# Two-scale attention with a gated convolution on one core: the mask of the local scores as eight products on the scores' own tiles

## The chip, the core and the metric

The kernel runs on one core of one Trainium2 chip. A core has a matrix engine (TensorE, PE in the rows; its weight loads are PEld), VectorE (DVE), ScalarE (ACT), GpSimd (POOL) and SyncE (SP), which issues most transfers. Each engine works through its own queue in order and waits on semaphores for the others. Two on-chip memories matter: SBUF, from which all engines read, and PSUM, into which TensorE writes and from which VectorE and ScalarE read. The metric is the device time of one execution in microseconds (us).

## The reference: what is computed

Batch 8, 8 heads, 576 positions, head width 64. Each position attends to its neighbours nearer than four (local), and, over means of four positions, to the whole sequence (coarse). Their sum is multiplied with `w_val`, gated by a causal convolution of five taps, and multiplied with `w_out`.

```python
out_d = sm_attn(q_d, k_d, v_d)                  # q, k, v as means over 4 positions
out_up = np.repeat(out_d, factor, axis=2)
mask = np.abs(pos[:, None] - pos[None, :]) < factor
scores = scale * np.matmul(q, k.transpose(0, 1, 3, 2))
scores = np.where(mask, scores, -1000000000.0)
...
x = out_up + out_local                          # heads side by side: 512 columns
gate = 1.0 / (1.0 + np.exp(-gate_pre))          # gate_pre: 5 taps of x along the sequence
return gate * (x @ w_val) @ w_out
```

## The kernel before

The work is cut into 32 pairs: eight batches with four pairs of heads each (p = 4 * batch + pair). A pair passes through these steps, by the names that stand in the rows. `sl`: local scores on TensorE. The sequence is cut into 20 blocks of 29 queries, each with its 35 keys; a product has 64 rows (one head's width) and 29 columns of weights, so it takes a 64x32 tile of the array, eight of which stand side by side: two halves of the rows (one per head) and four groups of 32 columns. The scores lie in two PSUM banks (b = 0, 1), four groups of 32 partitions each. In the program there are 40 f32 products; the profile shows each as two rows, 80 in all. Then `mx`, `ex`, `sm`, `rs` (row maximum, difference, sum, reciprocal on VectorE, the exponential on ScalarE) and `pexp` (normalization, in two halves, on VectorE or GpSimd), `tl` (transposes on TensorE, copied to `pt` by ScalarE) and `x` (local output on TensorE). The coarse way: `half` and `qs` (sums over four positions for the first two batches, VectorE or GpSimd), `sd` (coarse scores), `cmx`, `cbi`, `pd`, `cs`, `crs` (softmax), `tc` (transposes, copied to `pdt`), `odp` (coarse output) and `od`. `xt` adds both. `xhs` and `xls` are x split into a high and a low part, `gp` is the convolution (a first tap on ScalarE, four on VectorE) and its gate. The projections work in blocks of 504 columns of the joined batches: `val` (16 groups per block, of three 504-column products: high by high, high by low, low by high), `h` (gate times val), `hhl` (h split in two), `out`, `ob` and the transfer to `out_t`. The weights come as f64 bit fields and are split on the chip (`raw`, `a_v`, `a_o`, `wl`).

The mask is added by TensorE itself. `lay` (L714 to L721) opens a pair's scores: for each of the two banks one bf16 product of the whole array, the identity (`ident_b`, 128x128) with 175 columns of `mask_b`, starts the sum in PSUM with -1e9 where a key doesn't count and 0 elsewhere. `mm` (L723) then adds the 80 score rows. The mask table (`_band_mask`) has one row per partition of the scores: query j of block parity e stands in row 32 * (hd + 2e) + j.

The order of all instructions is written out while the program is built. `tensor_order` (L488) gives TensorE's list from the tables `START`, `START3`, `START4` and `STEADY`, one entry per step, where `P` is one group of three projection products and a stroke behind a name means the pair before. `Planner` then plays the list through with a duration for every step (the numbers in each `op(...)`, `RESULT`, `switch`), takes a later entry of the list where the first one isn't ready, chooses VectorE, ScalarE or GpSimd where a step may run on several, and lets each engine's instructions be issued in the order that came out. A step that has `cols` may get dummies ahead of it (`keep_warm`, L589: bf16 products of a constant into a PSUM bank that is written anew afterwards), as many as `keep_busy` (L430) counts. Transfers into SBUF are sent by SP (`send`, L608), each waiting for the fourth before it (`PACE = 4`), in the order of `EARLY` at first. `QKSPLIT = 1` cuts q and k of pair 0 into two transfers (`qk_in`, L655).

## Time and profile before

| | before |
|---|---|
| runs without a profile, us | 375.63, 373.29, 371.87 (median 373.29) |
| profiled execution, us | 373.75 |
| its span (first to last instruction), us | 371.5 |
| busy in the span: TensorE, VectorE, ScalarE, GpSimd, us | 358.9, 304.9, 247.5, 91.1 |
| TensorE's granted clock, mean over the span | 0.999 |
| instructions | 14101 |

Busy time is what an engine's own instructions cover. Products on TensorE are pipelined and their ends are modelled, so rows of one engine overlap, and the step from one start to the next says more than a duration. Times in the rows count from the start of the span.

### The profile page before, as it was taken

The page shows a single profiled execution, that of the slowest core. Times are in us where ns is not written, and L with a number is a line of the kernel's source. Part 1 is how long each engine was busy: PE and PEld are TensorE (multiplying, and loading weights), DVE is VectorE, ACT ScalarE, POOL GpSimd, SP SyncE. Part 2 cuts the span into 40 slices and gives each one's busy share as a digit, 9 for nine tenths or more (in the row PEclk, how much of TensorE's full clock was granted, in tenths as well). Part 3 has the DMA queues.
Part 4 walks back from the last instruction along what each step waited for, and adds up shares of the span by engine and source line. Part 5 has one row for each costly group of instructions (what it writes and reads, how often), then busy time and mean ns, then how long its engine had stood idle before and what let it go on. Part 6 is the DMA issues. An engine that isn't in the chain of part 4 may idle for free.

```text
span 371.5 us, 14101 instructions
## 1 busy us (share of the span) xinstructions
PE 358.9 (97%) x6020; PEld 286.0 (77%) x6020; DVE 304.9 (82%) x673; ACT 247.5 (67%) x664; POOL 91.1 (25%) x116
## 2 busy tenths in 40 slices
PE   7899899998999999999999999999999999999996
PEld 4677676776777777777778787777777778778996
DVE  3988999998999989997999799879997999570520
ACT  2898798967875949674777587857874767422221
POOL 4211225741462116102522052203100320000000
PEclk9999999999999999999999999999999999999999
DMA  7899999999989969995799879892345101102012
GB/s 248 246 278 297 332 220 231 268 249 292 285 187 275 255 197 235 200 280 199 197 207 232 279 187 203 228 239 68 101 154 160 37 3 59 56 0 85 28 49 79
DMA packets 23550, 68.97 MB, mean 186 GB/s; under 512 B 2880, under 2 KB 8768, under 8 KB 23488
## 3 DMA queue, kind: packets, MB, share of 16 engines
q1 hardware_dynamic: 18592, 50.42, 42.0%
q0 software_dynamic: 4608, 17.50, 26.0%
q8 instruction: 47, 0.77, 0.9%
q10 hardware_dynamic: 288, 0.16, 0.2%
q14 instruction: 15, 0.12, 0.1%
HBM read 58.63 MB, written 9.44 MB: 183 GB/s over the span
## 4 chain that ended last, share of the span: by engine, by line
PE 75%; DMA 11%; DVE 9%; ACT 3%; issue 2%; POOL 0%; SPq 0%; DVEq 0%; ACTq 0%
PE val L1119 8%; PE val L1121 8%; PE val L1120 8%; PE out L1119 8%; PE out L1120 8%; PE out L1121 8%; DMA vg<-in_vg 6%; PE x L939 5%; PE sl L732 5%; PE odp L981 5%; PE tl L889 5%; PE tc L912 4%; DMA qk<-in_qk 3%; DVE gp L1030 3%; PE sd L809 3%; DMA out_t<-ob 2%
## 5 line engine op out<-in xcount | busy, mean ns | idle before, releaser
L1030 DVE SCALAR_TENSOR_TENSOR gp<-xt,cw,gp 128x576 f32<-128x576 f32 x128 | 106.0, 836 | 2.6 <-ACT gp L1024 2.4
L1119 PE MATMUL val<-xhs,wh_v 128*128 128x504 f32 (+1 forms) x160 | 63.2, 395 | 0.0
L1121 PE MATMUL val<-xls,wh_v 128*128 128x504 f32 (+1 forms) x160 | 59.6, 372 | 0.1
L1120 PE MATMUL val<-xhs,wl_v 128*128 128x504 f32 (+1 forms) x160 | 59.5, 372 | 0.0
L1119 PE MATMUL out<-hhl,wh_o 128*128 128x504 f32 (+1 forms) x144 | 57.6, 400 | 0.1
L1121 PE MATMUL out<-hhl,wh_o 128*128 128x504 f32 (+1 forms) x144 | 54.8, 380 | 0.0
L1120 PE MATMUL out<-hhl,wl_o 128*128 128x504 f32 (+1 forms) x144 | 54.7, 380 | 0.0
L1147 DVE SCALAR_TENSOR_TENSOR h<-gp,val 128x288 f32<-128x288 f32 (+6 forms) x64 | 26.7, 447 | 18.8 <-PE val L1121 18.5
L1211 ACT ACTIVATE ob<-out 128x504 f32<-128x504 f32 (+2 forms) x40 | 22.0, 551 | 24.7 <-PE out L1121 11.4
L832 ACT ACTIVATE pd<-sd,cbi 112x144 f32<-112x144 f32 x96 | 35.4, 380 | 1.6 <-DVE cbi L825 1.6
L1121 PEld LDWEIGHTS val<-xls,wh_v 128*128 128x128 f32 x160 | 30.1, 188 | 5.6 <-DVE xls L1013 0.5
L1119 PEld LDWEIGHTS val<-xhs,wh_v 128*128 128x128 f32 x160 | 30.1, 188 | 4.1 <-issue 0.2
L1120 PEld LDWEIGHTS val<-xhs,wl_v 128*128 128x128 f32 x160 | 30.2, 189 | 3.5
L1119 PEld LDWEIGHTS out<-hhl,wh_o 128*128 128x128 f32 x144 | 27.2, 189 | 5.8 <-issue 1.0
L1167 POOL TENSOR_TENSOR hhl<-h,hhl 128x504 fp32r<-128x504 f32 x15 | 19.2, 1278 | 49.9 <-DVE gp L1030 23.6
L1024 ACT ACTIVATE gp<-xt,cw 128x576 f32<-128x576 f32 x32 | 24.8, 776 | 9.5 <-DVE h L1147 7.4
L1121 PEld LDWEIGHTS out<-hhl,wh_o 128*128 128x128 f32 x144 | 27.1, 188 | 5.1
L1120 PEld LDWEIGHTS out<-hhl,wl_o 128*128 128x128 f32 x144 | 27.2, 189 | 3.8
L732 PEld LDWEIGHTS sl<-qk 64*29 64x29 f32 x2560 | 24.8, 103 | 6.9 <-issue 1.6
L1161 ACT CAST hhl<-h 128x504 fp32r<-128x504 f32 (+2 forms) x44 | 22.1, 521 | 11.9 <-DVE h L1147 11.9
L1009 ACT CAST xhs<-xt 128x576 fp32r<-128x576 f32 (+4 forms) x40 | 22.3, 577 | 11.7 <-DVE xt L950 11.4
L950 DVE TENSOR_TENSOR xt<-x,od 128x290 f32<-128x290 f32 x64 | 26.3, 450 | 4.6 <-PE x L939 3.3
(96 smaller groups left out, 731.5 us busy)
## 6 DMA issues: line engine op xcount, KB each, us to landing
qk<-in_qk SPq DMA_DIRECT2D x31, 586.0 KB, 5.6
qs<-in_qkr POOLq DMA_DIRECT2D x18, 576.0 KB, 7.9
vw<-in_vw SPq DMA_DIRECT2D x32, 320.0 KB, 5.9
out_t<-ob SPq DMA_DIRECT2D x32, 252.0 KB, 5.2
vs<-in_vgr POOLq DMA_DIRECT2D x21, 320.0 KB, 7.5
qs<-in_qkr SPq DMA_DIRECT2D x6, 576.0 KB, 7.4
vs<-in_vgr SPq DMA_DIRECT2D x7, 320.0 KB, 5.4
raw_v<-in_w_val SPq DMA_DIRECT2D x4, 512.0 KB, 6.0
```

Of the source, the lines that this page charges most:

```text
L732: nc.tensor.matmul(out=sc[32 * qd : 32 * qd + BQ, b, m * KW : (m + 1) * KW], lhsT=t[r, 0, 3 + blk : 3 + blk + BQ], rhs=t[r, 1, blk : blk + ...
L832: nc.scalar.activation(out=s["pd"][:, g], in_=s["sd"][:, g], func=AF.Exp, scale=1.0 / 128.0, bias=s["bi"][:, g : g + 1], accum_out=s["csm" ...
L950: nc.vector.tensor_tensor(out=s["xt"][:, 4:].rearrange("p (m a j r) -> p a m j r", m=NPR, a=2, r=2)[:, par], in0=s["x"][par].rearrange("p ...
L1009: nc.scalar.copy(out=xhs[:, c, g : g + t - f], in_=s["xt"][:, 4 + f : 4 + t])
L1024: nc.scalar.activation(out=s["gp"], in_=s["xt"][:, 4 : 4 + S], func=AF.Copy, scale=cw[:, c, 4:5])
L1030: return nc.vector.scalar_tensor_tensor(out=s["gp"], in0=s["xt"][:, k : k + S], scalar=cw[:, c, k : k + 1], in1=s["gp"], op0=ALU.mult, op1 ...
L1119: nc.tensor.matmul(out=o, lhsT=wh[:, d, col], rhs=his[d], start=d == 0, stop=False)
L1120: nc.tensor.matmul(out=o, lhsT=wl[:, d, col], rhs=his[d], start=False, stop=False)
L1121: nc.tensor.matmul(out=o, lhsT=wh[:, d, col], rhs=los[d], start=False, stop=d == NC - 1)
L1147: nc.vector.scalar_tensor_tensor(out=t["h"][:, cs], in0=st[b * NC + c]["gp"][:, f:e], scalar=1.0, in1=box["o"][:, cs], op0=ALU.add, op1=AL ...
L1161: nc.scalar.copy(out=t["hh"][:, cuts[n]], in_=t["h"][:, cuts[n]])
L1211: nc.scalar.mul(t["ob"][:, cs], box["o"][:, cs], 0.5)
```

## The change

The two mask products of the whole array become eight of a 64x32 tile each: every tile that will hold scores is started by a product of 64 rows of the identity, 32 of its columns, with 175 columns of the mask. The rows of the identity are chosen so that each tile takes its 32 mask rows out of its own half of the partitions, and the table of the mask is laid out anew for that. Mask and scores become one step (`sl`) in place of two (`mk`, `sl`), in the planner's tables too, with the duration 800 in place of 172 and 711 and 88 weight loads in place of 82. q and k of pair 0 come in one transfer.

```diff
-QKSPLIT = 1
+QKSPLIT = 0
...
-STEADY = "odp'' x'' sd tc1' tc0' P P P P mk sl tl1' tl0' P P P P"
+STEADY = "odp'' x'' sd tc1' tc0' P P P P sl tl1' tl0' P P P P"
...
-        def lay():
-            s["sc"] = sc = ps.tile([P, 2, 512], F32, tag="s", name=f"sl{p}", bufs=SB)
+        def mm():
+            t = s["qk"]
+            sc = ps.tile([P, 2, 512], F32, tag="s", name=f"sl{p}", bufs=SB)
             keep_warm(sc[:, 0])
             for b in range(2):
-                nc.tensor.matmul(
-                    out=sc[:, b, 0:n], lhsT=ident_b, rhs=mask_b[:, n * b : n * b + n], start=True, stop=False
-                )
-
-        def mm():
-            t, sc = s["qk"], s["sc"]
+                for qd in range(4):
+                    r = (LO, HI)[(qd + b) % 2]
+                    rows = r.start + 32 * (qd // 2)
+                    nc.tensor.matmul(
+                        out=sc[32 * qd : 32 * qd + 32, b, 0:n],
+                        lhsT=ident_b[r, rows : rows + 32],
+                        rhs=mask_b[r, n * b : n * b + n],
+                        start=True,
+                        stop=False,
+                    )
...
-            ("mk", p), "PE", 172, lay, [("qk", p)], banks=[("s", [("sub", p)])], cols=(350, 350), loads=2,
+            ("sl", p), "PE", 1300 if p < QKSPLIT else 800, mm, [("qk", p)],
+            banks=[("s", [("sub", p)])], cols=(1180, 350), loads=88,
         )
-        op(("sl", p), "PE", 1200 if p < QKSPLIT else 711, mm, [("qk", p), ("mk", p)], cols=(1050, 0), loads=80)
...
-                rows = [32 * (hd + 2 * e) + j for hd in range(2)]
+                rows = [32 * (e + 2 * half) + j for half in range(2)]
```

What this does to the order, at three places. First, TensorE at pair 10, as at nearly every pair behind it: the last projection product, mask, scores, transposes of the pair before. Before:

```order
L1121 MATMUL val1_2_1942<-xls_90,wh_v_96 128x504
L719 LDWEIGHTS ident_b_79
L719 MATMUL sl10_1976<-mask_b_91,ident_b_79 128x175
L719 LDWEIGHTS ident_b_79
L719 MATMUL sl10_1976<-mask_b_91,ident_b_79 128x175
L732 MATMUL sl10_1976<-qk10_1397 29x35 x40
L889 MATMUL tl9_1_2027<-ident_77,pexp1_81 128x128 x2
```

And of the change, where the pair of a load and a product stands eight times (once here):

```order
L1126 MATMUL val1_2_2011<-xls_90,wh_v_96 128x504
L723 LDWEIGHTS ident_b_79
L723 MATMUL sl10_2050<-mask_b_91,ident_b_79 32x175
...
L737 MATMUL sl10_2050<-qk10_1532 29x35 x40
L894 MATMUL tl9_1_2111<-ident_77,pexp1_81 128x128 x2
```

Six loads and six products more stand in a pair; what stands around them is the same. At pairs 17, 21 and 29 a group of the projection stood between mask and scores, and no longer does.

Second, TensorE in the opening, where the coarse and the local output of pair 3 are computed (`odp3`, `x3`; `vg3` is the part of v that they need, `const` marks a dummy). Before, with four dummies ahead of `odp3` and two ahead of `x3` (one of each here):

```order
L1121 MATMUL val0_1_898<-xls_90,wh_v_96 128x504
L809 MATMUL sd5_914<-qs1_722 64x144 x6
L592 LDWEIGHTS const-bfloat16-1.0
L592 MATMUL odp3_929<-const-bfloat16-1.0 128x144
...
L981 MATMUL odp3_929<-pdt3_853,vg3_540 64x144 x16
L592 LDWEIGHTS const-bfloat16-1.0
L592 MATMUL x3_964<-const-bfloat16-1.0 128x290
...
L939 MATMUL x3_964<-pt3_866,vw3_486 64x58 x20
```

And of the change, with twenty dummies ahead of `odp3` (one here):

```order
L1126 MATMUL val0_1_913<-xls_90,wh_v_96 128x504
L944 MATMUL x3_946<-pt3_892,vw3_513 64x58 x20
L592 LDWEIGHTS const-bfloat16-1.0
L592 MATMUL odp3_981<-const-bfloat16-1.0 128x144
...
L986 MATMUL odp3_981<-pdt3_879,vg3_581 64x144 x16
L894 MATMUL tl4_0_1034<-ident_77,pexp0_80 128x128 x3
L592 LDWEIGHTS const-bfloat16-1.0
L592 MATMUL sd5_1039<-const-bfloat16-1.0 128x350
L814 MATMUL sd5_1039<-qs1_742 64x144 x6
```

The coarse scores of pair 5 have gone from ahead of `odp3` to behind it, `x3` from behind it to ahead. In the whole program there are 90 dummies in place of 68, all but a few of them ahead of pair 5.

Third, GpSimd from pair 5 to pair 6 (its DMA rows are transfers that add into `qs` and `vs`). Before:

```order
L1100 TENSOR_TENSOR wl_o_99<-a_o2_1068,wh_o_98 128x512
L769 TENSOR_TENSOR pexp1_81<-ex1_83,rs5_1187 64x2x5x35
L634 DMA vs2_1039<-in_vgr 80x1024
L698 TENSOR_TENSOR half7_1_1303<-qk7_922 128x288
L634 DMA qs2_957<-in_qkr 128x1152
L1167 TENSOR_TENSOR hhl0_1_1294<-h0_1_1178,hhl0_1_1294 128x504
L634 DMA vs2_1039<-in_vgr 80x1024
L1167 TENSOR_TENSOR hhl0_2_1406<-h0_2_1391,hhl0_2_1406 128x504
L769 TENSOR_TENSOR pexp0_80<-ex0_82,rs6_1441 64x2x5x35
```

Of the change:

```order
L1105 TENSOR_TENSOR wl_o_99<-a_o2_1202,wh_o_98 128x512
L699 TENSOR_TENSOR qs1_742<-half7_1_1209 128x144
L634 DMA qs2_1063<-in_qkr 128x1152
L1172 TENSOR_TENSOR hhl0_1_1375<-h0_1_1207,hhl0_1_1375 128x504
L634 DMA vs3_1324<-in_vgr 80x1024
L774 TENSOR_TENSOR pexp0_80<-ex0_82,rs6_1424 64x2x5x35
```

The normalization of pair 5 and the low part `hhl0_2` are on VectorE now. In the same way the low parts of x of pairs 0 and 5 and the half normalization of pair 9 have gone to VectorE, that of pair 8 to GpSimd. After pair 9 half a normalization of pairs 10, 17, 19, 21 and 29, the coarse normalizations of pairs 13, 22, 24 and 25 and the low part of x of pair 20 have gone to VectorE, and four low parts of h, half a normalization of pair 23 and a coarse one (pair 11) have left it, net.

## Rows read from the trace of the kernel before

**Rows 1.** Windows by stage: stretch, us, busy (instructions), clock, DMA share, GB/s.

```profile
5.00:33.00 28.00, 24.20 (x595) 17.95 (x579) 24.30 (x62) 22.75 (x67) 4.74 (x6) 1.00 0.96 275
33.00:93.00 60.00, 55.54 (x1077) 42.45 (x1071) 58.07 (x124) 49.32 (x128) 24.02 (x29) 1.00 1.00 270
93.00:310.00 217.00, 217.00 (x3916) 172.17 (x3914) 198.00 (x444) 153.49 (x428) 58.70 (x62) 1.00 0.73 189
```

**Rows 2.** Timeline of TensorE, pair 20: start, us, engine, line, what, count, [idle before].

```profile
199.91 0.33 PE L719 MATMUL sl<-mask_b,ident_b 128*128 128x175 bf16 x2
200.17 0.89 PE L732 MATMUL sl<-qk 64*29 64x35 f32 x80
201.00 0.77 PE L889 MATMUL tl<-ident,pexp 128*128 128x128 f32 x5
...
203.87 0.39 PE L1120 MATMUL out<-hhl,wl_o 128*128 128x504 f32 x1
204.10 0.39 PE L1121 MATMUL out<-hhl,wh_o 128*128 128x504 f32 x1
204.42 0.71 PE L981 MATMUL odp<-pdt,vs 72*64 72x144 f32 x8
```

**Rows 3.** TensorE's groups by form: count | busy us, mean ns | idle before.

```profile
L809 PE MATMUL sd<-qs 64*64 64x144 f32 x384 | 17.3, 289 | 1.9 <-DVE qs L699 0.9 <-DVE ex L747 0.7 <-DVE xt L950 0.3
...
L592 PE MATMUL odp<-const-bfloat16-1.0 128*128 128x144 bf16 x12 | 1.5, 231 | 0.0
```

**Rows 4.** Timeline of TensorE: the coarse scores of pairs 26 and 27.

```profile
253.66 0.92 PE L809 MATMUL sd<-qs 64*64 64x144 f32 x24
254.51 0.39 PE L912 MATMUL tc<-ident_s,pd 112*72 112x112 f32 x2
```

**Rows 5.** Timeline of SP: issues of q and k of pair 0, and of v.

```profile
0.74 1.30 SPq L609 DMA_DIRECT2D qk<-in_qk  x2
...
5.35 0.34 SPq L609 DMA_DIRECT2D vg<-in_vg  x1
```

**Rows 6.** The page's transfers: count, KB each, median us from issue to landing.

```profile
qk<-in_qk SPq DMA_DIRECT2D x1, 296.0 KB, 3.9
```

**Rows 7.** Timeline of TensorE in the opening.

```profile
4.66 1.30 PE L732 MATMUL sl<-qk 64*29 64x35 f32 x80
...
43.84 0.43 PE L592 MATMUL odp<-const-bfloat16-1.0 128*128 128x144 bf16 x4
44.20 2.18 PE L981 MATMUL odp<-pdt,vg 72*64 72x144 f32 x32
...
68.01 0.31 PE L592 MATMUL out<-const-bfloat16-1.0 128*128 128x350 bf16 x1 [0.65 <-DVE h L1147]
...
90.43 0.32 PE L719 MATMUL sl<-mask_b,ident_b 128*128 128x175 bf16 x2 [0.57 <-ACT pd L832]
...
92.89 0.30 PE L592 MATMUL tc<-const-bfloat16-1.0 128*72 128x336 bf16 x1 [0.53 <-ACT pt L894]
```

**Rows 8.** Timeline of VectorE in the opening.

```profile
33.26 0.46 DVE L698 TENSOR_TENSOR half<-qk 128x288 f32<-128x288 f32 x1 [1.03 <-DMA qk<-in_qk]
...
78.51 1.56 DVE L1030 SCALAR_TENSOR_TENSOR gp<-xt,cw,gp 128x576 f32<-128x576 f32 x1
```

**Rows 9.** VectorE's groups by form, columns as in rows 3.

```profile
L1030 DVE SCALAR_TENSOR_TENSOR gp<-xt,cw,gp 128x576 f32<-128x576 f32 x128 | 106.0, 836 | 2.6 <-ACT gp L1024 2.4
L769 DVE TENSOR_TENSOR pexp<-ex,rs 64x350 f32<-64x350 f32 x51 | 27.8, 545 | 1.1
...
L1013 DVE TENSOR_TENSOR xls<-xt,xhs 128x576 fp32r<-128x576 f32 x18 | 13.6, 754 | 3.9 <-ACT xhs L1009 3.9
...
L1167 DVE TENSOR_TENSOR hhl<-h,hhl 128x504 fp32r<-128x504 f32 x9 | 6.0, 671 | 0.7 <-ACT hhl L1161 0.7
```

**Rows 10.** Timeline of GpSimd beside the tap at 78.51 us of rows 8.

```profile
78.02 1.43 POOL L1013 TENSOR_TENSOR xls<-xt,xhs 128x576 fp32r<-128x576 f32 x1 [0.65 <-DVE xls L1013]
```

More of the change, by code (lines that the diff above doesn't have):

```diff
@@ L110 @@
 COLS = 3400
-START = "mk sl tl0' tl1' sd tc1' tc0' odp' x'"
-START3 = "tl1' sd mk sl tl0' tc0' tc1' x' odp'"
-START4 = "mk sl tc0' tl1' P tl0' sd tc1' odp' x' P P P"
-STEADY = "odp'' x'' sd tc1' tc0' P P P P mk sl tl1' tl0' P P P P"
+START = "sl tl0' tl1' sd tc1' tc0' odp' x'"
+START3 = "tl1' sd sl tl0' tc0' tc1' x' odp'"
+START4 = "sl tc0' tl1' P tl0' sd tc1' odp' x' P P P"
+STEADY = "odp'' x'' sd tc1' tc0' P P P P sl tl1' tl0' P P P P"
 AHEAD = "0.0 0.1 1.0 1.1"
@@ L173 @@
 class Planner:
[L177 removed]
+    RESULT = {"sl": 223, "sd": 211, "tc": 198, "tl": 200, "odp": 213, "x": 345}
     PIECE = {"DVE": 105, "ACT": 151, "POOL": 200, "PE": 0}
@@ L225, in lat @@
         return self.CROSS[e].get(to, 200)
-    SHAPE = {"P": "full", "mk": "full", "tc": "turn", "tl": "turn", "odp": "half", "x": "four", "sd": "four", "sl": "eight"}
+    SHAPE = {"P": "full", "tc": "turn", "tl": "turn", "odp": "half", "x": "four", "sd": "four", "sl": "eight"}
     def switch(self, a, b):
```

1 line of the change is left out of this document (removed).

## Prediction, written before the changed kernel ran

> **What bounds the kernel now.** I read the busy times by stage first [rows 1]. From 93 to 310 us TensorE is busy in all of 217.00 us, at a granted clock of 1.00, which is its 2.4 GHz level; VectorE is busy for 198.00 of them, ScalarE for 153.49. TensorE sets the pace there: what an edit takes out of its stream comes off the end, until VectorE's 19 us of slack are used up. From 33 to 93 us it is mixed: VectorE 58.07 of 60 us, the DMA engines at a share of 1.00, TensorE 55.54. From 5 to 33 us the DMA share is 0.96 and no compute engine is full. The change therefore has a place that I can price (TensorE's stream from about 53 us on, where the weights' products have begun to fill it) and a place that I can only bound (the opening).
>
> Then the timeline of TensorE around one pair's scores [rows 2]. Rows overlap, since the end of a product is modelled, so I price by start to next start. The two mask products start at 199.91, the scores at 200.17, the transposes at 201.00: 0.26 us for the mask, 0.83 us for the 80 score rows. A 504-column product takes 0.23 us to the next one (203.87 to 204.10), which is 0.45 ns per column, so the mask's two times 175 columns are 0.158 us. The remaining 0.10 of the 0.26 is the turn from the whole array to tiles of 64x32. The same turn shows elsewhere: the last 504-column product before the coarse output takes 0.32 us to its successor (204.10 to 204.42) and not 0.23, so 0.09.
>
> **The change part by part.**
>
> *The mask, per pair.* Out go two whole-array products, 0.158 us. In come eight products of 175 columns, each on its own 64x32 tile. The turn of 0.10 us stays: it moves from behind the mask to ahead of it. So a pair gains 0.158 less what the eight cost. No row of before has a bf16 product on such a tile, so I bound it. If the tiles work at once, the eight cost the longer of one stream (175 x 0.45 ns = 0.079 us) and eight issues at the scores' own pace (0.83 us / 80 = 10.3 ns each, 0.082 us). If four work at once they cost 0.158, and the gain is nil; if two, 0.316; if one, 0.63.
> Which is nearer? An f32 product of 144 columns has a modelled time of 289 ns, a bf16 dummy of as many columns 231 ns [rows 3]: f32 needs 58 ns more, hence about twice the 0.45 ns, some 0.85 ns per column. The coarse scores run 24 products of 144 columns on four 64x64 tiles between 253.66 and 254.51 [rows 4]: one after the other that would be 24 x 0.122 = 2.9 us, and it is 0.85, so about 3.5 of four tiles work at once. The local scores are 80 x 35 x 0.85 ns = 2.4 us in 0.83, about three at once, held back by their 10.3 ns per issue. Long streams fill their tiles, and 175 columns are long. I take 0.09 us: the gain is 0.07 us a pair, with ends 0.079 and 0.
> It counts for pairs 5 to 31, whose scores stand where TensorE is full or nearly so: 27 x 0.07 = 1.9 us, ends 0 and 2.1. For pairs 0 to 4 it disappears in waits.
> The Trainium skill, "TensorE: Matmul & The Clock Gate", section "Back-to-back issue gap", has a floor of about 25 ns from one product's start to the next however few the columns. By it the eight would cost 0.20 us and each pair lose 0.04, some 1.1 us in all, which is a time of 375.7 with the opening's term below. The scores' 10.3 ns per product on the same eight tiles speak against it here.
>
> *One piece for mask and scores.* Both pieces waited for the same tile of q and k, and nothing new is waited for. In the place where a projection stood between mask and scores (three later pairs), one more turn of 0.09 us falls away; I leave these 0.3 us in the margin. Behind the piece the transposes and projections wait for nothing else. The 12 more instruction rows per pair on TensorE cost their issue, which the 10.3 ns hold already.
>
> *Pair 0's q and k in one transfer.* The first half's issue starts at 0.74 us and the two issues take 1.30; the first transfer of v goes out at 5.35, on the second half's landing [rows 5]. The second half (296 KB) landed 3.9 us after its issue [rows 6], at about 5.3. One transfer has the same bytes, starts at 0.74 and lands between 4.7 (an issue of 0.6 us saved) and 5.4. Scores of pair 0 start before that today, at 4.66, but take 1.30 us [rows 7], since their last part waits for the second half; in one go they are 0.9 us from landing. So their end moves by -0.3 to +0.3 us. The three transfers behind it on SP's queue are issued 0.6 us earlier or more; from the first of v on each waits for the fourth before it, and that lands as today. I price it at 0: VectorE waits for a later q and k at 33.26 after 1.03 us idle [rows 8], so what is won or lost before is swallowed there; ends -0.3 and +0.5.
>
> *The moved order.* The opening's order is another on every engine, up to about pair 10. Two things can be counted.
> First, dummies ahead of the coarse output of pair 3: 20 products of 144 columns now, 4 before. Four took 0.36 us (43.84 to 44.20) [rows 7], so 16 more are 1.4 us, less two dummies that fall away ahead of x3 (0.35 at most): +1.1 us if TensorE could have worked there, 0 if it waits anyway. I take the middle, +0.5.
> Second, VectorE takes work from GpSimd. Up to pair 9, net: two low parts of x (0.75 us each), one normalization (0.55) and one low part of h (0.67) [rows 9], 2.7 us; the sums of q and k that change sides nearly cancel. But GpSimd's work holds VectorE up: a convolution tap, 0.84 us in the mean [rows 9], took 1.56 us at 78.51, beside a low part of x on GpSimd from 78.02 [rows 8, 10]. Two low parts of x less on GpSimd give back about 1.4 us. Net 1.3 us, of which a part falls before 33 us, where VectorE has 3.7 us free. I take +0.4 for the end; ends 0 and 2.7. On the other side the new order may lose gaps of the old: TensorE waited 0.65 us at 68.01, 0.57 at 90.43, 0.53 at 92.89 [rows 7], 1.75 us.
> After pair 9 VectorE gets some 2.2 us more in the same way (four normalizations, three coarse ones and a low part of x, less four low parts of h), against 19 us of slack; I price that at 0, and if the slack is in the wrong place it is 2.2 us.
>
> **Sum.** 373.75 us for the profiled execution (span 371.5 and 2.25 around it): -1.9 (mask) + 0 (transfer) + 0.9 (opening) = 372.75. That execution is 0.46 us above the median of the runs shown, 373.29; from the median it would be 372.3. I forecast **372.5 us**. The ends together: 373.75 - 2.1 - 1.75 - 0.3 = 369.6, and 373.75 + 1.1 + 2.7 + 0.5 = 378.05 with nothing gained.
>
> **The rivals.**
> *The opening costs more than the mask gives.* Place: pairs 3 to 9. For it: VectorE is at 58.07 of 60 us there, it gets more work, and the 20 dummies are on TensorE's queue whether or not it waits. Against: GpSimd's hold-ups shrink with the work. Price +2.5 to +3.8 (both terms whole): 373.75 - 1.9 + 2.5 = 374.4, to 375.7.
> *The opening gains.* The old gaps of 1.75 us close and the dummies hide: 373.75 - 1.9 - 1.75 = 370.1, to 371.5 with half of it.
> *The mask products do not run eight at once: slower than before.* Place: every pair's scores. With two at once each pair loses 0.158 us, 27 x 0.158 = 4.3: 373.75 + 4.3 + 0.9 = 379; one at a time 0.47 x 27 = 12.8: 387. It decides from 0.158 us for the eight on (no gain) and is visible above 0.30 us. For it: no bf16 product on tiles is in the trace, and the local scores fill only three of eight tiles. Against: the coarse scores fill 3.5 of four.
> *The change does nothing:* four at once, gain nil, opening as forecast: 374.6.
>
> **How the numbers follow.** Chances: forecast (371.5 to 374.0) 0.52, opening dearer 0.18, opening gains 0.17, mask not at once 0.08, no gain 0.05. A measurement of this kernel can tell about 1% (3.7 us) from no change: 369.6 to 377.0. Below lies the far end of the opening's gain, 0.09; above the mask rival and the far end of the dear opening, 0.13; between 0.78. The range 369.8 to 377.2 leaves out the mask rival, 0.08, and the two far ends, about 0.1.
>
> **What would show it.** Mask start to first score start plus the turn ahead: 0.18 to 0.20 us if I am right, over 0.26 if not. Scores 0.83 as before. Steps of TensorE from pair to pair after 93 us shorter by 0.07. TensorE gapless from pair 10 on. Dummies before the output of pair 3: whether TensorE's rows before them show a wait. The mask of pair 20, at 199.91 before [rows 2], tells opening and mask together: fifteen pairs' gain of 1.05 against 0.9 of the opening puts it at 199.8. A wait of TensorE on VectorE after 110 us would make the sum wrong, and so would mask products that start 20 ns or more apart.

## The result, and the profile after

| | before | after |
|---|---|---|
| median of the runs timed beside each other, us | 374.28 (371.87 to 375.77, 6 runs) | 370.21 (369.77 to 370.98, 6 runs) |
| ratio, with its 95% interval | | 0.9896 (0.9856 to 0.9936) |
| profiled execution, its span, us | 373.75, 371.5 | 370.79, 369.0 |
| busy: TensorE, VectorE, ScalarE, GpSimd, us | 358.9, 304.9, 247.5, 91.1 | 356.8, 305.3, 247.4, 82.4 |
| instructions | 14101 | 14510 |

The change is worth 1.0%, 4.07 us between the medians. The forecast was 372.5 with a range of 369.8 to 377.2; the time lies at the lower end of the range, below the forecast's own case (371.5 to 374.0), and the gain is about four times the 1.0 us that was forecast (373.75 to 372.75). Here and below a median is over all executions of a kernel, a ratio over those within 1.5% of its fastest.

Busy time by stage, to be held against [rows 1] (span of the stretch, then busy time and instructions of PE, PEld, DVE, ACT, POOL, granted clock, DMA share, GB/s):

```profile
5.00:33.00 28.00, 25.31 (x669) 19.17 (x670) 25.82 (x69) 22.47 (x66) 2.84 (x5) 1.00 0.99 291
33.00:93.00 60.00, 57.17 (x1103) 43.97 (x1101) 57.59 (x127) 50.24 (x132) 21.70 (x27) 1.00 1.01 264
93.00:310.00 217.00, 215.26 (x4093) 171.60 (x4092) 200.06 (x451) 155.08 (x433) 54.21 (x54) 1.00 0.72 190
```

Two things stand out. TensorE is busier in the opening (57.17 of 60 us, 55.54 before; about 1 us of that is dummies, of which twenty take 1.41 us below where four took 0.36). And it is no longer gapless behind 93 us: 215.26 of 217.00.

The timeline of TensorE shows both the mask and the gaps (start, duration, engine, line, operation; in brackets the idle time before and what ended it):

```profile
17.94 0.63 PE L737 MATMUL sl<-qk 64*29 64x35 f32 x49 [0.91 <-issue]
...
23.72 0.46 PE L986 MATMUL odp<-pdt,vg 72*64 72x144 f32 x4 [0.73 <-issue]
...
41.86 0.45 PE L944 MATMUL x<-pt,vw 64*64 64x58 f32 x14 [0.76 <-issue]
42.24 1.48 PE L592 MATMUL odp<-const-bfloat16-1.0 128*128 128x144 bf16 x20
43.65 2.18 PE L986 MATMUL odp<-pdt,vg 72*64 72x144 f32 x32
...
157.98 0.39 PE L1126 MATMUL out<-hhl,wh_o 128*128 128x504 f32 x1
158.31 0.27 PE L723 MATMUL sl<-mask_b,ident_b 64*32 64x175 bf16 x8
158.39 0.88 PE L737 MATMUL sl<-qk 64*29 64x35 f32 x80
159.20 0.77 PE L894 MATMUL tl<-ident,pexp 128*128 128x128 f32 x5
...
196.17 0.39 PE L1126 MATMUL out<-hhl,wh_o 128*128 128x504 f32 x1
196.49 0.27 PE L723 MATMUL sl<-mask_b,ident_b 64*32 64x175 bf16 x8
196.58 0.77 PE L737 MATMUL sl<-qk 64*29 64x35 f32 x67
198.61 0.29 PE L737 MATMUL sl<-qk 64*29 64x35 f32 x13 [1.26 <-issue]
198.82 0.77 PE L894 MATMUL tl<-ident,pexp 128*128 128x128 f32 x5
...
245.92 0.33 PE L737 MATMUL sl<-qk 64*29 64x35 f32 x23 [0.48 <-issue]
```

Pair 16 (158.31) is the undisturbed case: 0.33 us from the last projection product to the mask, 0.08 for the eight mask products, 0.81 for the scores. Pair 20 answers [rows 2]: the same 0.09 for the mask, and then, with 67 of 80 score rows done, TensorE stands still for 1.26 us and waits for nothing that the profile shows. Five such gaps sum to 4.14 us; before there was one, 0.16 us at 18.79.

Where the 2.96 us between the two profiled executions went, read from the start of the mask of pairs 10 and 31: after is 2.11 us ahead at pair 10 (100.92 against 103.03), gains 0.29 from there to pair 31 (2.03 us of gain less 1.74 us of gaps), and 0.56 behind it, most of that around the span.

### The profile page after: what moved, and what is told of

It reads as the page before. It is cut to its first block, busy times and chain, and to the rows that moved or that the text cites. A ratio compares the mean times of both kernels' runs of the same rounds, so it can differ in the third digit from the quotient of the medians.

```text
span 369.0 us, 14510 instructions
## 1 busy us (share of the span) xinstructions
PE 356.8 (97%) x6234; PEld 285.6 (77%) x6234; DVE 305.3 (83%) x682; ACT 247.4 (67%) x667; POOL 82.4 (22%) x106
## 4 chain that ended last, share of the span: by engine, by line
PE 86%; DMA 6%; ACT 3%; issue 3%; DVE 1%; ACTq 0%; DVEq 0%
PE val L1124 9%; PE val L1126 9%; PE val L1125 9%; PE out L1124 8%; PE out L1125 8%; PE out L1126 8%; PE odp L986 7%; PE x L944 6%; PE tc L917 5%; PE sl L737 5%; PE tl L894 5%; PE sd L814 3%; DMA out_t<-ob 3%; DMA vs<-in_vgr 2%; PE sl L723 2%
## 5 line engine op out<-in xcount | busy, mean ns | idle before, releaser
L1172 POOL TENSOR_TENSOR hhl<-h,hhl 128x504 fp32r<-128x504 f32 x18 | 22.7, 1262 | 58.6 <-DVE gp L1035 42.3
L924 ACT COPY pdt<-tc 72x336 f32<-72x336 f32 x64 | 25.2, 436 | 10.8 <-PE tc L917 10.4
L737 PE MATMUL sl<-qk 64*29 64x35 f32 x2560 | 28.7, 200 | 2.6 <-issue 2.6
L760 ACT ACTIVATE ex<-ex 128x350 f32<-128x350 f32 x32 | 16.1, 505 | 21.9 <-DVE ex L752 21.9
L774 DVE TENSOR_TENSOR pexp<-ex,rs 64x350 f32<-64x350 f32 x56 | 29.6, 529 | 1.2
```

Source lines behind the costliest of these rows:

```text
L737: nc.tensor.matmul(out=sc[32 * qd : 32 * qd + BQ, b, m * KW : (m + 1) * KW], lhsT=t[r, 0, 3 + blk : 3 + blk + BQ], rhs=t[r, 1, blk : blk + ...
L774: return eng.tensor_tensor(out=px[r].rearrange("p (m b) k -> p b m k", b=2)[:, :, :, BQ * e : BQ * e + KW], in0=s["ex"][r].rearrange("p (b ...
L924: nc.scalar.copy(out=s["pdt"][:, kb], in_=s["tc", kb])
L1172: return eng.tensor_tensor(out=t["hl"][:, cs], in0=t["h"][:, cs], in1=t["hh"][:, cs].bitcast(F32), op=ALU.subtract)
```

## What the gaps are

The page counts the transfers that bring the engines' instructions (queue, then transfers, MB, share of the DMA engines); before it was 47 transfers and 0.77 MB:

```profile
q8 instruction: 49, 0.80, 0.9%
```

TensorE has 6234 pairs of a weight load and a product, so each of the 49 transfers of 16 KB brings some 127 of them: a page. I numbered TensorE's products in the order of the records and looked where the gaps stand. In all 14 profiles of this study there are 36 gaps with "issue" of 0.16 us and more, and each stands 2 to 8 products behind a member of the row 94, 221, 348, ..., a step of 127 (the offset grows along the program, as missing records and semaphore instructions would make it). Each ends 1.2 to 1.6 us after an instruction packet has landed. At pair 20 the packet begins at 196.15 and takes 0.93 us; the scores go on at 198.61.

So TensorE has run to the end of a page and waits for the next: a code gap. The packet is asked for about when the page ahead of it is entered: where the DMA engines are idle it begins 0.6 us behind that in the middle of 63 cases, where they are full 2.7 us behind, up to about 5 (186 cases, six profiles; with missing records a single value is off by some tenths). Begin plus 1 us for the packet plus 1.4 us: a page that TensorE uses up in 5 us, because the 88 pairs of a scores step lie in it, can be too short. This was in sight ahead of the prediction: the planner has constants for it (`PAGE, FIRSTPAGE = 127, 94`, a `FETCH` time and a function `fetched` that counts `loads`), and the diff raises `loads` from 82 to 88.

The Trainium skill, "Runtime: NRT & Kernel Launch", section "Instruction fetch mechanics", says that instructions come in 16 KiB blocks, the next one fetched while the current one runs, and that the cost of crossing into the next is mostly hidden. The 16 KB agree with the packets here; the hiding does not hold for this kernel, whose gaps cost 4.1 us.

## Experiments

They ran in three sets on three chips, each set beside the kernel before on the same chip. Ratios are against that kernel there, with their 95% interval; between sets only ratios are compared.

### One part of the change at a time

**Only the eight mask products, in the old order** (`m8_old_order`): the kernel before with

```
-                nc.tensor.matmul(
-                    out=sc[:, b, 0:n], lhsT=ident_b, rhs=mask_b[:, n * b : n * b + n], start=True, stop=False
-                )
+                for qd in range(4): ...   # the eight products of the change
...
-                rows = [32 * (hd + 2 * e) + j for hd in range(2)]
+                rows = [32 * (e + 2 * half) + j for half in range(2)]
```

> The kernel before with one edit: the mask as eight products on 64x32 tiles (and its rows laid out for them), a piece of its own as before; order of all engines, transfers and dummies untouched. Price theory (the eight cost 0.09 us, the turn only changes places): mask start to first score 0.16 to 0.20 us less the turn, so each pair 0.07 us shorter where TensorE is full; the end 1.9 us earlier, 371.9 us against 373.75, ratio 0.995, with no new gap on TensorE. Code theory (TensorE's instructions arrive in pages of some 127 load-and-product pairs, as the five 'issue' gaps of the changed kernel suggest): the same 0.07 us a pair, but 192 more pairs make 1.5 more pages and move all boundaries, so new 'issue' gaps of 0.3 to 1.3 us appear, each 2 to 3 us behind a transfer of the instruction queue; 1 to 4 us of gaps, a time of 372.5 to 376.

Measured: 375.02 us, ratio 1.0005 (0.9967 to 1.0043). The steps are shorter as forecast (pairs 11 to 19: 76.72 us, before 77.58, 0.107 a pair), and the time is the same. Six of these eight steps are shorter by 0.05 to 0.13 us; the other two nearly cancel (at pair 11 the coarse scores of before ran 0.42 us longer than elsewhere, and pair 17, below, is 0.21 longer now). The timeline shows what took it back in this execution, and the granted clock by stretch what followed:

```profile
199.41 0.47 PE L1126 MATMUL out<-hhl,wh_o 128*128 128x504 f32 x1
202.46 0.39 PE L1127 MATMUL out<-hhl,wl_o 128*128 128x504 f32 x1 [2.57 <-issue]
...
203.38 0.39 PE L1128 MATMUL out<-hhl,wh_o 128*128 128x504 f32 x1
...
204.69 0.62 PE L1126 MATMUL out<-hhl,wh_o 128*128 128x504 f32 x1
205.11 0.62 PE L1127 MATMUL out<-hhl,wl_o 128*128 128x504 f32 x1
```

```profile
202.00:204.00 2.00, 1.54 (x7) 1.28 (x7) 1.90 (x6) 0.90 (x2) 0.00 (x0) 0.95 0.92 213
204.00:206.00 2.00, 2.00 (x6) 1.17 (x4) 0.26 (x1) 0.00 (x0) 0.77 (x1) 0.50 0.96 344
206.00:208.00 2.00, 2.00 (x50) 1.47 (x49) 0.00 (x0) 0.99 (x2) 0.00 (x0) 0.70 0.31 119
```

A gap of 2.57 us for a page, and behind it the clock at 0.50 (1.2 GHz): a 504-column product takes 0.42 us to the next, not 0.23.

A second execution of the same kernel (`m8_look`):

> A second execution of the kernel before with the eight mask products, for its gaps only. Its mask gain of 0.09 us a pair stands in the steps of its first trace (pair 11 to 19: 76.72 us against 77.58), but not in its median (375.02 against 375.2). If the gaps in code supply take it back, this execution too shows 2 us or more of 'issue' gaps (with the loss of clock behind a long one), where the kernel before showed 0.16; if not, under 0.5, and the loss has another place.

It had only 0.23 us of such gaps, so the expectation of 2 us or more fell. From the mask of pair 10 to that of pair 31 it took 201.61 us, before 202.68: half of the 2 us that the mask gives in the new order. At pairs 17, 21 and 29 a projection stands between mask and scores in this order, and the array turns to tiles, back and again to tiles:

```profile
170.82 0.27 PE L722 MATMUL sl<-mask_b,ident_b 64*32 64x175 bf16 x8
171.02 0.49 PE L1126 MATMUL val<-xhs,wh_v 128*128 128x504 f32 x1
...
171.90 0.89 PE L739 MATMUL sl<-qk 64*29 64x35 f32 x80
```

From this mask to the next takes 10.91 us, with mask and scores in one piece 10.62 (the changed kernel); with the old mask it is 10.70 in two pieces (before) and 10.72 in one (`m2_new_order`). So the one piece is part of the gain, some 0.28 us at each of three pairs, but only together with the new mask. The rest was lost ahead of pair 10, which stands at 105.02: the first 4 MB are in at 17.5 us here (16.4 in `m8_old_order`). Gaps take the gain back in one execution and the opening in another.

**Only the old mask, in the new order** (`m2_new_order`): the changed kernel with the two whole-array products and the old table, as one piece with the scores (the diff above, read backwards).

> The changed kernel with the old mask: two products over the whole array, in one piece with the scores, and the old mask rows; order, dummies and transfers as in the changed kernel. Price theory: each pair from 5 on is 0.07 us longer, 1.9 us in all, 372.7 us, with gaps as in the changed kernel. Code theory: 192 fewer pairs, so boundaries move and the gaps of 0.91, 0.73, 0.76, 1.26 and 0.48 us leave their places; with half of their 4.1 us gone the time is 370.3 to 371, with none gone 372.7. The opening: if its lead of 2.1 us at pair 10 comes from the order, 1.7 us of it is here too (mask of pair 10 at 101.3); if it comes from the mask, none (103).

Measured: 374.25 us, ratio 0.9978 (0.9944 to 1.0013). Pairs 10 to 31 take 202.74 us without a code gap. The opening had one of 2.75 us at 32.67, with the clock at 0.50 from 34 to 36 us, and pair 10 stood at 103.13. That is the place for a lead that comes from the mask, but the gap and the slow clock ahead of it cost at least as much as the lead, so it doesn't decide; and the time is above both forecasts (370.3 to 372.7). Against the changed kernel's ratio below (0.9916, on another chip), the new mask in this order is worth 0.6%, some 2.3 us; forecast were 1.9.

**q and k of pair 0 in two transfers, order made anew** (`two_parts`, `QKSPLIT = 1` in the changed kernel), and **in one transfer, with the old mask** (`one_part_old_mask`, `QKSPLIT = 0` in the kernel before):

> The changed kernel with q and k of pair 0 in two transfers again (the planner makes another order from it). If the one transfer is what made the opening gain, the lead at the mask of pair 10 (103.03 us before, 100.92 after) falls back by 1 to 2 us, to 102 to 103, and the time is 371.5 to 373. If the transfer is worth nothing and the gain is the planner's luck with the rest of the order, the mask of pair 10 can stand anywhere between 100 and 103 whatever pair 0 does, while the scores of pair 0 end within 0.5 us of the changed kernel's.

> The kernel before with q and k of pair 0 in one transfer and the old mask (the planner makes another order from it). If the transfer made the opening's gain: mask of pair 10 at 101 to 101.5 instead of 103.03, time 371.7 to 372.3. If it is worth nothing by itself: mask of pair 10 within 0.5 us of 103, time 373.3 to 374.3; a shift of either sign by over 0.5 us with pair 0's scores unmoved would say that the order behind it decides.

Measured: 375.27 us, 1.0014 (0.9977 to 1.0051), and 374.68, 0.9988 (0.9946 to 1.003). The opening of the second is that of the changed kernel (pair 10 at 100.92), as the transfer theory wanted; its profiled execution, 370.98 us, is the fastest of its 12, and its median is no better than before. The first has pair 10 at 105.6, past both expectations, with a code gap of 3.29 us at 44.78.

Neither half of the change alone moves the median; both together do. So I measured the whole again, and the transfer within the new order.

**The changed kernel again** (`after_again`):

> The changed kernel itself, unedited, beside the kernels below and 5 rounds of the kernel before: what the whole change is worth where the other experiments were timed. Sum of what the traces show so far: 0.09 us a pair from the mask (27 pairs, 2.4 us) and some 2 us of the opening, which is 371 us against 375.2, ratio 0.989. If the profile of the change was a lucky execution (spans of one kernel differ by some us with the gaps in TensorE's instruction supply), the ratio is 0.995 or more. In its trace every gap called 'issue' on TensorE should end 1.2 to 1.6 us behind the landing of an instruction packet, whatever its place in the program.

Measured: 371.72 us (370.06 to 372.53), ratio 0.9916 (0.9888 to 0.9943): the gain is there in a second measurement too. Pair 10 stands at 101.05, within 0.13 us of the first profile. Five gaps of 4.38 us in all: three at the steps where the first profile had them (18.17, 41.71 and 246.99), two at new ones (11.57, 63.52). The largest, at pair 25:

```profile
245.10 0.28 PE L737 MATMUL sl<-qk 64*29 64x35 f32 x9
246.99 0.33 PE L737 MATMUL sl<-qk 64*29 64x35 f32 x23 [1.61 <-issue]
```

**Two halves inside the same step, new order kept**, once with both halves counted in the window of four transfers (`halves_counted`), once with the second alone (`halves_one`):

```
+                if p == 0:
+                    send(out=s["qk"][:, :, 0 : SQ // 2], in_=qk[b, c][:, :, 0 : SQ // 2])
+                    send(out=s["qk"][:, :, SQ // 2 : KS], in_=qk[b, c][:, :, SQ // 2 : KS])
+                    return
```

(in `halves_one` the first is `nc.sync.dma_start`, which doesn't count).

> The changed kernel, with q and k of pair 0 sent in two halves inside the same step; each half counts in the window of four transfers, as before the change; every other engine's order as in the changed kernel. If the one transfer made the opening's gain: DMA rate from 4 to 8 us falls from 415 GB/s back to 300 to 350, the first 4 MB are in at 16.4 us instead of 14.2, the mask of pair 10 comes 1.5 to 2 us later (102.5 to 103), the time grows by 1.5 to 2 us. If the order of the engines made it: 4 MB at 16.4 perhaps, but the mask of pair 10 stays at 100.9 to 101.4 and the time within 0.5 us of the changed kernel's.

> As the kernel with two halves, but the first half does not count in the window, so that the fourth whole transfer (the first weights) may be issued without waiting for it. Window theory (the change's worth is one more transfer in flight from the start): 400 GB/s or more from 5 to 8 us, 4 MB in at 14.2 to 14.8 us, mask of pair 10 and time as in the changed kernel. Row theory (shorter rows of the halves make the transfers slow): 300 to 350 GB/s from 4 to 8 us, 4 MB at 16 us or later, as with both halves counted.

Measured: 375.67 us, 0.9992 (0.9948 to 1.0037), and 375.82, 1.0017 (0.9974 to 1.006). Against 0.9916 that is 0.8 to 1.0%, some 3 to 4 us, for one edit of a transfer. The stretches at the start, first of the changed kernel, then of the two others (last columns: granted clock, DMA share, GB/s):

```profile
4.00:8.00 4.00, 3.51 (x166) 2.31 (x166) 2.85 (x7) 0.49 (x1) 1.48 (x8) 1.00 1.04 414
0.00:14.00 14.00, 11.70 (x280) 7.42 (x280) 8.77 (x24) 7.26 (x19) 5.16 (x23) 1.00 0.84 281
```

```profile
10.00:12.00 2.00, 1.36 (x8) 0.94 (x7) 1.96 (x7) 0.15 (x3) 0.29 (x1) 0.81 0.85 219
12.00:14.00 2.00, 2.00 (x16) 1.12 (x15) 1.19 (x5) 2.00 (x4) 0.14 (x1) 0.50 0.59 154
4.00:8.00 4.00, 3.31 (x115) 1.93 (x113) 2.45 (x6) 0.49 (x1) 0.83 (x7) 1.00 0.86 272
0.00:14.00 14.00, 11.03 (x227) 6.54 (x228) 6.83 (x19) 5.18 (x13) 5.18 (x23) 0.90 0.74 220
```

```profile
4.00:8.00 4.00, 2.83 (x106) 1.82 (x105) 2.28 (x6) 0.34 (x1) 0.83 (x7) 1.00 0.95 319
0.00:14.00 14.00, 10.16 (x232) 6.13 (x233) 7.12 (x19) 6.14 (x15) 5.18 (x23) 1.00 0.77 239
```

From 4 to 8 us the changed kernel moves 414 GB/s, the others 272 and 319, at DMA shares of 1.04, 0.86 and 0.95. In 14 us that is 3.9 MB against 3.1 and 3.3; the first 4 MB are in at 14.2, 16.7 and 16.1 us. One more transfer in flight (319 against 272) gives a third of it back; the rest stays away, and 319 GB/s and 16.1 us are what the row theory forecast.

Its reason is not shown, though. The halves go out in packets of 1160 and 1184 bytes, the whole in packets of 4688, and by the records of the queue the halves' packets are through at 4.8 us: from 4 to 8 us they are 13% and 9% of the bytes. A DMA engine moved the 1160-byte packets at 17 and 19 bytes per ns, the 1184-byte ones at 21, the 4688-byte ones at 22. What is slower is the traffic behind them: the 128 packets of 2560 bytes of the first `vw`, the same in all three kernels, take 103 ns each in the changed kernel, 162 and 156 ns in the two others. What slows them stays open. The Trainium skill, "Perfetto Trace Analysis", section "DMA Optimizations", says that DMAs under 2 KB carry a marked overhead per transfer; the times of the short packets show little of it here, and not the step from 414 to 272 and 319 GB/s.

With both halves counted there is a second loss: TensorE is busy for 1.36 us between 10 and 12 us, and the granted clock is 0.50 from 12 to 14 us. Pair 10 is at 106.36 and 105.91. The bigger part of these 5 us comes later, where `odp` of pair 4 waits 3.11 and 3.55 us for its `vs` (1.11 in the changed kernel), with the clock at 0.50 from 60 to 64 us behind it; the new order was planned for data that comes sooner, so these two runs may overstate the transfer's worth.

```profile
59.23 1.23 PE L990 MATMUL odp<-pdt,vs 72*64 72x144 f32 x8 [3.11 <-DMA vs<-in_vgr]
```

```profile
60.04 1.23 PE L990 MATMUL odp<-pdt,vs 72*64 72x144 f32 x8 [3.55 <-DMA vs<-in_vgr]
```

The granted clock of every execution, which is on record, says how much. In the executions that the ratios use it is 0.980 to 0.995 and 0.986 to 0.999 in the two kernels, 0.995 to 1.000 in the changed kernel. At 0.50 a 504-column product took 0.42 us in place of 0.23, above, so where TensorE sets the pace a mean clock below 1 loses about (1 - clock) times the span, 3.7 us for 0.01; this is an estimate. By their times the two kernels are 2.9 and 3.4 us behind the changed kernel in the mean, less this loss 0.3 and 0.9 us. By this estimate most of what the halves cost is slow clock behind the waits that they bring, and little is the later data by itself.

### What makes the gaps

**Less data on the DMA engines** (`light`): `more()`, which sends the accumulating transfers of q, k and v, sends nothing; the sums over four rows keep the first row only.

```
-                nc.gpsimd.dma_start(out=u[nm], in_=src[b, r], accum_op=ALU.add)
+                pass
```

> The changed kernel without the accumulating transfers on GpSimd's queue (the sums over four rows of q, k and v for the coarse attention keep the first row only): 17 MB less over the DMA engines, TensorE's program, its pages and its order unchanged. Contention theory (an instruction packet stands behind data on the DMA engines): from 93 to 230 us a packet begins 0.7 to 1.5 us after TensorE enters the page ahead of it, where it was 2.4 us in the mean and up to 5; no 'issue' gap above 0.2 us after 93 us; and the times of one kernel's executions, which scatter over 5 us or more, lie within 2 us. Own-pace theory (the supply is slow by itself, or the gap belongs to the scores): gaps of 0.5 us and more remain at dense steps, the scatter stays. Time: 366 to 369, since the opening also gets its data sooner.

Measured: 368.7 us median (365.8 to 372.06, 4 runs), ratio 0.9814 (0.976 to 0.9868). TensorE's program is the same, and its stretch from 93 us on is full again, at half the DMA share (0.91 in the changed kernel over these 137 us):

```profile
93.00:230.00 137.00, 137.00 (x2642) 109.54 (x2638) 128.77 (x294) 98.31 (x276) 22.17 (x20) 1.00 0.48 150
```

No gap with "issue" in the whole execution. Between 93 and 230 us an instruction packet begins 0.45 us behind the page's entry in the mean and 1.55 at most (21 packets), in the second profile of the changed kernel 2.03 and 4.7 (20 packets). So the wait for a page is a wait behind data. The four executions still spread over 6 us, where 2 were expected, and the granted clock on record tells what spreads them: 365.8 and 366.87 us at 1.000, 370.53 at 0.989, 372.06 at 0.986. Less the estimated loss of (1 - clock) times the span, from above, they are 365.8, 366.9, 366.5 and 366.9: without the clock they lie within 1.1 us. What brought the slow clock in two of them, their one trace (of the first) can't show.

**The page boundaries shifted** (`phase64`, `phase32`): more dummies ahead of the scores of pair 0.

```
         n = min(WARM, bank.shape[1])
-        for _ in range(plan.warm):
+        more = 0 if first_warm.pop("done", 1) else 64
+        if more:
+            n = 110
+        for _ in range(plan.warm + more):
```

> The changed kernel with 64 more dummies ahead of the scores of pair 0 (76 of 110 columns in place of 12 of 350, so that they end before the mask's data lands); nothing else moves, no row that computes is touched. It shifts each page boundary of TensorE's program by 64 pairs. Code theory: every 'issue' gap stands at a boundary of the shifted lattice (product 30, 157, 284 and so on, a step of 127, in place of 94, 221, 348), 1.2 to 1.6 us behind an instruction packet's landing; the gaps at 17.9, 41.8 and 246 us that both executions of the changed kernel had are gone from there, and others appear: likeliest near 8 us (2.4), 20, 32 and 36 us (1 to 2 each), 187 and 207 us (0.8 to 1.4). The fetch delays seen so far, laid on that lattice, make 1.6 times the gaps of the unshifted one: 6 to 7 us for 4.1 to 4.4, and a gap of over 2.5 us may bring the clock down as well; time 373 to 377. Place theory (the gap belongs to the scores of certain pairs): gaps stay at 17.9, 41.8, 198 or 246 us and the time within 0.7 us of the changed kernel's 371.7.

> As the kernel with 64 more dummies, with 32 more (44 of 192 columns in place of 12 of 350): boundaries at product 62, 189, 316 and so on. Code theory: gaps on that lattice, likeliest near 8 us (2.5), 21.5 us (1.3), 34 and 39 us (0.8 each), 53 us (1.1), 149 us (0.9), 168 us (1.05); 1.45 times the gaps of the unshifted kernel, 6 us, time 372.5 to 376. Place theory: as the changed kernel, 371.7 within 0.7.

Measured: 373.77 us (371.81 to 376.36), ratio 0.9966 (0.9929 to 1.0004), and 372.41 (371.71 to 374.12), 0.9889 (0.9807 to 0.9972), beside 376.18 of the kernel before. The gaps of the first, on TensorE:

```profile
8.80 0.50 PE L741 MATMUL sl<-qk 64*29 64x35 f32 x34
12.64 0.74 PE L741 MATMUL sl<-qk 64*29 64x35 f32 x46 [3.34 <-issue]
...
37.58 0.34 PE L948 MATMUL x<-pt,vw 64*64 64x58 f32 x7 [0.82 <-issue]
...
42.95 0.25 PE L741 MATMUL sl<-qk 64*29 64x35 f32 x3 [1.43 <-issue]
```

They stand at products 223, 732 and 860, counted with the new dummies: the same row as ever, and so 64 products earlier in the work. The scores of pair 1, without a gap in the changed kernel, now have one of 3.34 us; those of pairs 2, 20 and 25, which had one, have none. Behind the 3.34 us the clock stays at 0.50 from 12 to 16 us. With 32 the gaps are at products 223 (1.53 us), 860 and 4547. They sum to 5.59 and 3.28 us, where 6 to 7 and 6 were expected, and most of the places that were named had none. The place theory is out by the places. The times say less: 0.9966 is 0.5% above the changed kernel's 0.9916, with intervals that just overlap, and 0.9889 is not above it at all, so shifting by 32 cost nothing that can be measured. Both also started late, which I hadn't meant: the 76 dummies took 5.49 us, not 3.5 as by 0.42 ns per column; the unedited ones at the start take 3.66 us for 12 of 350, 0.87 ns per column.

### The price of the mask by itself

`mask_twice`: the eight products made twice, the second time adding.

```
-            for b in range(2):
+            for b, again in ((0, 0), (1, 0), (0, 1), (1, 1)):
...
-                        start=True,
+                        start=not again,
```

> The changed kernel with the eight mask products made twice (the second eight add the mask again, which masks the same scores). Price theory: eight more cost 0.09 us (11 ns each); mask start to first score 0.36 us where it is 0.27 now with its modelled end (by starts: 0.18 us for sixteen, 0.09 for eight). If the eight of the changed kernel were hidden behind the turn, sixteen cost 0.16 to 0.2 more. Its 256 more pairs make two more pages, and gaps at other places; the time itself is not read.

```profile
164.67 0.39 PE L1126 MATMUL out<-hhl,wh_o 128*128 128x504 f32 x1
164.99 0.35 PE L723 MATMUL sl<-mask_b,ident_b 64*32 64x175 bf16 x16
165.15 0.88 PE L737 MATMUL sl<-qk 64*29 64x35 f32 x80
165.96 0.76 PE L894 MATMUL tl<-ident,pexp 128*128 128x128 f32 x5
```

Sixteen take 0.16 us where eight take 0.09 (0.162 and 0.086 in the median of the pairs), with 0.32 ahead and 0.81 behind as at pair 16. Eight more cost 0.08 us, 10 ns each, and nothing is hidden in the turn.

### The openings side by side

| kernel | first 4 MB in, us | mask of pair 10, us | pairs 10 to 31, us | code gaps before 93 us, sum (longest) | code gaps after | stretches with the clock at 0.50 to 0.60 |
|---|---|---|---|---|---|---|
| before | 16.4 | 103.03 | 202.68 | 0.16 | 0 | none |
| after | 14.2 | 100.92 | 202.39 | 2.40 (0.91) | 1.74 | none |
| after_again | 13.9 | 101.05 | 203.32 | 2.77 (1.12) | 1.61 | none |
| m2_new_order | 14.2 | 103.13 | 202.74 | 3.09 (2.75) | 0 | 34 to 36 |
| one_part_old_mask | 14.6 | 100.92 | 202.41 | 2.14 (1.81) | 0 | none |
| m8_old_order | 16.4 | 102.17 | 206.01 | 0 | 2.97 | 204 to 206 |
| two_parts | 16.9 | 105.60 | 202.25 | 4.23 (3.29) | 0 | 12 to 14, 46 to 48 |
| phase64 | 14.6 | 108.62 | 200.22 | 5.59 (3.34) | 0 | 12 to 18, 96 to 100 |
| light | 15.2 | 98.13 | 200.22 | 0 | 0 | none |
| m8_look | 17.5 | 105.02 | 201.61 | 0.23 | 0 | none |
| halves_counted | 16.7 | 106.36 | 200.56 | 0.56 | 0.99 | 12 to 14, 60 to 66 |
| halves_one | 16.1 | 105.91 | 202.10 | 1.10 | 1.84 (0.98) | 58 to 64 |
| phase32 | 14.2 | 104.91 | 201.72 | 2.46 (1.53) | 0.82 | 12 to 16 |
| mask_twice | 14.7 | 107.20 | 201.81 | 5.91 (2.47) | 0 | 14 to 16 |

The column of pairs 10 to 31 tells the mask's worth once more: 200.22 us with the new mask in the new order and no gap (twice), 202.68 and 202.74 with the old. In each of the last two one step is 0.4 to 0.5 us longer than its like; without that the difference is 2.0 us for 21 pairs, 0.10 each. Code gaps are not all that lengthens this stretch: `two_parts` has none in it and takes 202.25, with TensorE waiting 1.27 us for a coarse normalization on GpSimd at 242.28, and `after_again` has a wait of 0.69 us on ScalarE's `pt` at 240.46 beside its gap. `mask_twice`, without a gap in this stretch, takes 201.81: 1.59 more for 21 pairs, 0.08 each. Where the clock is slow ahead of pair 10, behind a code gap or a wait for data, the pair stands at 103.13 to 108.62; where it isn't, at 98.13 to 103.03, but for `m8_look` at 105.02, whose data came latest.

## Why the prediction was right, and where it was not

**The mask: right.** Forecast 0.09 us for the eight, 0.18 to 0.20 with the turn. Measured 0.086 and, with 0.09 of turn (0.32 less the usual 0.23), 0.17 to 0.18. From the last projection product to the transposes a pair takes 1.22 us (157.98 to 159.20), and took 1.32 in [rows 2] (from 0.23 us ahead of the mask at 199.91 to 201.00). I had 0.07 for the gain; it is 0.10. The products themselves give the 0.07 (0.158 for 0.086); the rest are terms that I had left unchanged, a turn of 0.09 in place of 0.10 and scores of 0.81 in place of 0.82 to 0.83. Both rivals on the mask (not eight at once, no gain) are out: products 20 ns apart would have made 0.16 us. The Trainium skill, "TensorE: Matmul & The Clock Gate", section "Back-to-back issue gap", with its floor of about 25 ns, would have made 0.20 us of the eight, as an estimate; the measured 0.09 contradicts it on these tiles.

**The turn: right.** It is 0.09 us ahead of the mask, where it was 0.10 behind. But the 0.3 us that I left in the margin for a turn falling away at three pairs do not exist: with the old mask the projection between mask and scores cost no turn of its own (10.70 us a step with it, 10.72 without). It is the new mask that would have paid for it.

**"The 12 more instruction rows per pair on TensorE cost their issue, which the 10.3 ns hold already": wrong.** The step that failed is that instructions cost only their issue. They also cost their supply. Gaps of 4.1 to 4.4 us came with the change, 1.6 to 1.7 of them behind pair 10, where nothing absorbs them; they took most of the 2.0 us that the mask gave between pairs 10 and 31. I cannot say that the 12 rows alone made them, since order and boundaries moved as well.

**"and that lands as today. I price it at 0": wrong,** and the largest error. I had compared when q and k of pair 0 land, and taken it that the transfers behind them follow as before. They don't; the issues on SP, to be held against [rows 5]:

```profile
0.74 0.37 SPq L609 DMA_DIRECT2D qk<-in_qk  x1
1.18 0.41 SPq L609 DMA_DIRECT2D vw<-in_vw  x1
1.64 0.42 SPq L609 DMA_DIRECT2D qk<-in_qk  x1
2.11 0.43 SPq L609 DMA_DIRECT2D raw_v<-in_w_val  x1
4.71 0.34 SPq L609 DMA_DIRECT2D vg<-in_vg  x1
```

Four whole transfers are on their way at 2.5 us, the first of v goes out 0.64 us sooner, and all of them move at a higher rate: in the first 14 us 281 GB/s, before 239, which is 0.6 MB more. What I called swallowed by VectorE's wait at 33.26 [rows 8] was not: 8 MB are in at 28.3 us, before at 30.6, and the mask of pair 5 starts at 48.57, before at 52.64. Within the new order this edit is worth 0.8 to 1.0%, by the estimate above mostly through the clock; it was forecast at 0, with ends of -0.3 and +0.5 us.

**The opening, +0.9: wrong in sign.** It came out at about -1.6 (-2.11 at pair 10, of which the mask is 0.5). The twenty dummies ahead of `odp3` took 1.41 us (42.24 to 43.65), as priced; whether TensorE could have worked there wasn't tested, since every edit of the dummies moves the pages too. VectorE, which was to pay 0.4 us for GpSimd's work, was busy 57.59 us from 33 to 93, before 58.07, and TensorE's idle time there fell from 4.46 us to 2.83 (about 1 us of it filled by the dummies). I take it that the data that came 2 us sooner outweighed both terms: `one_part_old_mask`, in yet another order, has the same lead. That the order had no part in it is not shown.

**The rivals.** The case that came is "the opening gains", 370.1 to 371.5 us, with 0.17; but not for the reason given there. Of the old gaps of [rows 7] the later two shrank only (0.32 at 88.71, 0.42 at 91.02), and a new one of 1.11 us stands at 55.93.

**The sum by its terms** (profiled executions): 373.75, -2.11 to pair 10 (in it 0.5 of the mask), -2.03 from pair 10 to 31, +1.74 of gaps there, -0.56 behind: 370.79. Forecast: -1.9 and +0.9. The number was close by luck: a gain that I hadn't seen (the transfer) and a cost that I hadn't seen (the supply of instructions) stood against each other. These terms add up between two executions, 2.96 us apart; the other 1.1 us between the medians (374.28 and 370.21) lies within the spread of the kernel before (371.87 to 375.77) and has no term of its own.

**The signs I had named.** Mask and turn of 0.18 to 0.20: 0.17 to 0.18, at the edge. Scores of 0.83: 0.81 where no gap falls in. Shorter steps: yes. No wait of TensorE on VectorE after 110 us: yes. TensorE gapless from pair 10: no. The mask of pair 20 at 199.8: it came at 196.49 and 196.94, 3 us sooner, and that is where the opening's term shows its wrong sign.

**What stays open.** Mask alone and transfer alone leave the median where it was (1.0005, 0.9988), and both together give 0.9896 and 0.9916; the two prices add up in the traces, not in the medians. The clock tells a part: less the estimated loss of (1 - clock) times the span, the mean of the executions that the ratios use is 0.4 us below that of the kernel before for the mask alone, 1.2 for the transfer alone, 3.1 for both. Even so the parts don't make the whole. Of the same executions, those of the kernels with halves or with the old mask spread over 4.5 to 5.6 us (7 to 32 each), those of the changed kernel over 1.2 and 2.5 (6 each), which may be for their fewer number: `phase64`, with ten, spreads over 4.6. Long gaps with the slow clock behind them, which none of the changed kernel's two profiles has, are in several of the others' and would do this, but each trace is one execution, and the kernel before had none in its own.

## What to carry to other kernels

Where a dense stream of small products is the bound, count its instructions as bytes too: find the transfers of the instruction queue in the profile, number the products, and see whether a page runs out while the DMA engines are full; a gap with "issue" at a constant step of products is that, and it moves when anything ahead of it adds an instruction. A transfer at the start is not priced by when its own data lands but by the rate that all transfers behind it get: look at GB/s at an equal DMA share, and at the time that packets of one size take. And an edit that saves 0.1 us in each of 32 steps is proven in the steps; the total may hide it, so measure both.

## What the runs showed of the hardware that I had not expected

- TensorE's instructions come in packets of 16 KB, 127 pairs of load and product from boundary to boundary; the packet for the next page begins 0.6 us after the page ahead of it is entered when the DMA engines are idle and 2.7 us (up to about 5) when they are full, and work goes on 1.2 to 1.6 us after it has landed (36 gaps of 0.16 to 3.34 us).
- Behind the code gaps of 2.47 us and more, five in these traces, the granted clock fell to 0.50 each time and stayed there for some 3 to 7 us; behind 2.16, 1.81 and 1.61 us (43.80 us of `mask_twice`, 52.37 of `one_part_old_mask`, 246.99 of `after_again`) it stayed at 1.00, behind 1.53 us (11.73 us of `phase32`) it was 0.55 to 0.60 over the next 4 us.
- Eight bf16 products of 175 columns on eight 64x32 tiles take 0.086 us and sixteen 0.162, 10 to 11 ns each, the pace of the 35-column f32 rows.
- The same 2560-byte packets took 103 ns each behind one transfer of q and k and 156 to 162 ns behind its two halves (414 GB/s from 4 to 8 us, against 319 and 272, at DMA shares of 1.04, 0.95 and 0.86). The 1160-byte packets of the halves moved at 17 to 19 bytes per ns of an engine, 4688-byte ones at 22.
- The four executions of `light` lie within 1.1 us once (1 - granted clock) times the span is taken off, and over 6 us as they are.
